# First batch's token products: the part over its first two token tiles and first 256 columns in a job between the two halves

## The chip, the cores and the metric

The kernel runs on one core of a Trainium2 chip. The metric is device time in microseconds (us) of one launch, from first to last instruction with what the launch adds around them. Three runs of the kernel before took 819.28, 820.15 and 820.51 us; the median is 820.15 us.

The engines are called here: PE (TensorE, matrix multiplies and transposes), DVE (VectorE), ACT (ScalarE), POOL (GpSimd) and SP (the queue that issues the transfers). Each takes its own list of instructions in the order in which they are written, and waits for the others through semaphores.

## The reference

Four batches (B = 4) of 576 tokens by 512 channels pass through three layers.

```python
# 1. attention, 8 heads of 64, only scores not below the 32nd largest of a row are kept
scores = q @ k.T / sqrt(64)
kth    = np.partition(scores, -32, axis=-1)[..., -32:-31]
attn   = softmax(where(scores >= kth, scores, -1e9))
x      = (attn @ v), heads joined                       # 576 x 512
# 2. gate: causal convolution over 5 tokens, sigmoid, times x @ w_val, then w_out
x      = (sigmoid(conv(x)) * (x @ w_val)) @ w_out
# 3. phase mixer
theta  = x @ w_theta
zr, zi = x * cos(theta), x * sin(theta)
y      = w_tok_r @ zr + w_tok_i @ zi                    # products over tokens
u      = x + y
out    = u + max(u @ w_ch, 0)
```

The change concerns the line of `y`, for the first batch.

## The kernel before, in words

**Attention.** A head pair has nine tiles of up to 128 query rows (`seq`, line 132). Batch 0 is split (`SPLIT = (0,)`, line 41): its four head pairs are run first for token tiles 0 and 1 (columns 0 to 255, half x = 0), then for tiles 2, 3 and the remaining 64 rows (columns 256 to 575, half x = 1). `COLS` (line 110) holds the two column ranges, `SETS` (line 1053) the token tiles of each half.

The loop at line 1373 takes one tile per step. In a step the functions of `SOON` or `STEP` (lines 58 to 60) are called in a fixed order, and each writes its instructions: `scores_pe` (PE, three steps ahead, into `ps`), `scores_out` (ACT copies `ps` to `s`, line 572), `pick` (DVE, eight largest values of six stretches, lines 594 to 600), `count` (ACT, line 607, which needs the `tops` that `pick` made), `below` (POOL, line 615), `rest` (DVE, line 621), `expo` (ACT, line 202), `mask` (DVE, line 676), `turn` (PE transposes into `pt`) and `turn_out` (ACT copies `pt` to `pT`, line 708). `close` ends a part: sums of the rows, the product of `pT` with v into `px` (line 780), and on DVE `px` times the reciprocal sums `rb` into `xT` (line 798).

**The layers behind.** They are generators in the list `jobs`: `front` (w_val, w_out, theta, and the products z of x with cosine and sine, DVE line 990) and `back` (token products into `py`, line 1134; channel product `ph`; output). `work` runs the first job of the list while `owed` nanoseconds last; a job says what it costs and pauses with `yield paid()`, or stops the step with `yield "sync"` when something isn't there. The budget of a step comes from `target`, which walks a list of `stages` (line 1215), each a cost and a fixed budget (`HIGH` = 6000) or the base of 4150. A job hands instructions for DVE and ACT to `later`; `run_later` writes them into the next step.

**What sets the order.** DVE and ACT have the order in which the program writes (`FIXED`, line 33). PE, POOL and SP are ordered by a scheduler from the priorities of the instructions. Whatever sets it, the order is fixed before the launch, and an engine does not skip an instruction that waits.

**Buffers.** Matrix results of the layers (`px`, `pconv`, `pval`, `pth`, `py`, ...) take turns in four banks (tag `m`), scores in two banks (`s`), transposes in two (`pt`).

**Token products before.** In `back(0)` each of the four channel groups m and each column half h gets one accumulation of nine matrix products, four over token tiles 0 and 1 (z_0) and five over tiles 2, 3 and the rest (z_1). A row group of such products carries f32 operands; the trace shows each as two rows. The token weights w_tok come as 128-row pieces that are converted by ACT, DVE and POOL while attention runs, one piece every two steps; `lacking` counts those not yet there.

Of the kernel before, what the change touches and what calls it, by code (L numbers as in the profile page):

```python
# [11 lines left out]
F32 = mybir.dt.float32  # L12
# [5 lines left out]
ALU = mybir.AluOpType  # L18
# [22 lines left out]
SPLIT = (0,)  # L41
# [49 lines left out]
def mixer(ctx, tc, qT, kT, vt, w_val, conv_t, w_out, w_theta, w_tok, w_ch, out, flag):  # L91
# [269 lines left out]
    def weights():  # L361
        half = DM
        W["raw"] = [ml.tile([P, half, 2], I32, tag=t, name=f"raw_{t}") for t in RAWS]
        W["tmp"] = [ml.tile([P, half], F32, tag=f"lo{x}", name=f"tmp{x}") for x in range(2)]
        pieces = []
        for name, src, factor in (("conv", conv_t, None), ("val", w_val, None), ("out", w_out, None),
                                  ("theta", w_theta, 1.0 / (2.0 * math.pi)), ("tok", w_tok, None), ("ch", w_ch, None)):
            rows, n = src.shape
            W[name] = cp.tile([P, -(-rows // P), n], F32, tag=f"w_{name}", name=f"w_{name}")
            words = src.bitcast(I32).rearrange("r (n t) -> r n t", t=2)  # L370

            chunks = -(-rows // P)
            cuts = [(c, 1, o, o + half) for c in range(chunks) for o in range(0, n - half + 1, half)]
            cuts += [(c, min(8, chunks - c), n // half * half, n) for c in range(0, chunks, 8) if n % half]
            for c, a, o, e in cuts:
                src = words[c * P : (c + a) * P, o:e].rearrange("(a p) n t -> p a n t", a=a)
                lacking[name] = lacking.get(name, 0) + 1
                pieces.append((name, W[name][:, c : c + a, o:e], src, factor, len(pieces)))
        return pieces


# [130 lines left out]
    def after(*keys):  # L512
        while not done.issuperset(keys):
            yield "sync"
# [208 lines left out]
    def close(part):  # L723
# [88 lines left out]
        cw = W["conv"]  # L812
        if hp == NP - 1:
            jobs.append(front(b, (x,) if split else (0, 1)))
            if x:
                jobs.append(back(b))
        yield
# [272 lines left out]
    def fine_tok(w):  # L1090
# [9 lines left out]
        fine["tok", w] = both  # L1100
        halve(*both, W["tok"][:, w, :], ("tok", B - 1, w))

    def back(b):
        x2T = ms.pop(b)

        def y_out(m, h, ps):
            lo, hi = COLS[h]

            def f():
                nc.vector.tensor_tensor(x2T[:, m, lo:hi], ps, x2T[:, m, lo:hi], ALU.add)  # L1110
                if m == NC - 1 and (h or b == B - 1):
                    for k in (h,) if b == B - 1 else range(2):
                        halve_room(b, k, "U", x2T)
                if not h:
                    due.append(m)
                    while due and m % 2 and not lacking["ch"]:
                        want(b, "ch", due.pop(0))
            return f

        due = []  # L1120
        while lacking["tok"]:
            yield "sync"
        if b < B - 1:
            for h, m in [(h, m) for h in range(2) for m in range(NC)]:
                lo, hi = COLS[h]
                yield from after(*[("z", b, i) for i in SETS[0]])
                ps = ps_m.tile([P, hi - lo], F32, tag="m", name=f"py_{b}_{m}_{h}")
                for x in range(2):
                    if x:
                        yield from after(*[("z", b, i) for i in SETS[1]])  # L1130
                    for i in SETS[x]:
                        zs = [(cos_of(b, i), i), (sin_of(b, i), i + NF + 1)] if i < NF else [(sin_of(b, i), NF)]
                        for k, (z, w) in enumerate(zs):
                            nc.tensor.matmul(ps, z[:, m * P : (m + 1) * P], W["tok"][:, w, lo:hi],  # L1134
                                             start=(i + k == 0), stop=(i == NF))
                            owe[0] += (hi - lo) * 1.675
                            if owe[0] >= GRAIN and i < NF:
                                yield paid()
                later.append(y_out(m, h, ps))
                yield paid()  # L1140
        else:
            for h in range(2):
                lo, hi = COLS[h]
                ps = [ps_m.tile([P, hi - lo], F32, tag="m", name=f"py_{b}_{m}_{h}") for m in range(NC)]
                for x, n in ((0, 0), (1, 0), (0, 1), (1, 1)):
                    for m in range(NC):
                        for i in SETS[x]:
                            for k, (_, w) in enumerate(mixed(b, i)):
                                yield from after(("cs"[k], b, i), ("tok", b, w))
                                z = fine_z(i, k)[n][:, m * P : (m + 1) * P]  # L1150
                                for t in fine["tok", w][: 2 - n]:
                                    first = (x, n, i, k) == (0, 0, 0, 0) and t is fine["tok", w][0]
                                    nc.tensor.matmul(ps[m], z, t[:, lo:hi], start=first, stop=n == 1 and i == NF)  # L1153
                                owe[0] += (hi - lo) * 0.425 * (2 - n)
                                if owe[0] >= GRAIN and i < NF:
                                    yield paid()
                        if x and n:
                            later.append(y_out(m, h, ps[m]))
                        yield paid()

        def h_out(m, h, ps):
            lo, hi = COLS[h]

            def f():
                nc.vector.scalar_tensor_tensor(x2T[:, m, lo:hi], ps, 0.0, x2T[:, m, lo:hi], ALU.max, ALU.add)
                n = b + 1
                if h and n in THREE:
                    if m % 2:
                        want(n, "val", m)
                    if (n * NP + m, 0) in there:  # L1170
                        split_x(n, m, 0)
                done.add(("o", b, m, h))
            return f

        def store(i, w, po):
            def f():
                ot = x2T[:w, :, i * P : i * P + P] if w == P else x2T[:w, :, :P]
                nc.scalar.copy(ot, po[:w])
                nc.sync.dma_start(out[b, i * P : i * P + w, :].rearrange("t (c w) -> t c w", c=NC), ot)
            return f  # L1180

        def turned(tiles):
            for i in tiles:
                w = P if i < NF else REM
                po = ps_m.tile([P, NC, P], F32, tag="m", name=f"po_{b}_{i}")
                for c in range(NC):
                    nc.tensor.transpose(po[:w, c, :], x2T[:, c, i * P : i * P + w], ident)
                later.append(store(i, w, po))
                yield 450

        while lacking["ch"]:
            yield "sync"
        while due:
            want(b, "ch", due.pop(0))
        for h, m in [(h, m) for h in range(2) for m in range(NC)]:
            lo, hi = COLS[h]
            yield from after(*halved(b, h, "U"), ("w", b, "ch", m))
            ps = ps_m.tile([P, hi - lo], F32, tag="m", name=f"ph_{b}_{m}_{h}")
            yield from products(ps, [(mat(b, "ch", m, c), chunk(b, h, "U", c)) for c in range(NC)])
            later.append(h_out(m, h, ps))  # L1200
            if (h, m) == (1, NC - 1):
                used(b, "ch")
            yield paid()
            if h and m == 1:
                yield from after(*[("o", b, c, 0) for c in range(NC)])
                yield from turned([0, 1])
        yield from after(*[("o", b, c, 1) for c in range(NC)])
        yield from turned(range(2, NF + 1))
# [7 lines left out]
    for b in range(B):  # L1216
        late = b == B - 1
        f = 1.275 if b in THREE else 1.675
        by = 0 if late else end((b + 1) * NP + 1, 0) + SHIFT[0]
        if b in SPLIT:  # L1220
            for x, (lo, hi) in enumerate(COLS):
                stages.append((2 * NC * (hi - lo) * NC * f + len(SETS[x]) * (NC * DM * f + 500.0), HIGH if x else None, by))
        else:
            stages.append((2 * NC * S * NC * f + 5 * NC * DM * f, HIGH if late else None, by))
        stages.append((NC * S * NC * 1.275 + 36 * S * 1.675 + 5000, HIGH if late else None,
                       0 if late else end((b + 2) * NP - 1, 1) + SHIFT[1]))
    spent_on = [0.0]

# [201 lines left out]
```

## Time and profile before

| | |
|---|---|
| median of three runs | 820.15 us |
| the profiled execution, its own time | 818.77 us |
| its span, first to last instruction | 817.0 us |
| PE busy | 722.8 us (88% of the span) |
| DVE busy | 665.9 us (82%) |
| ACT busy | 633.6 us (78%) |
| POOL busy | 451.4 us (55%) |
| the chain that ended last | PE 43%, DVE 30%, ACT 13%, POOL 6%, DMA 4% |

The busy shares are averages. In the chain that ended last DVE and PE take turns, so a stretch has to be read by itself: which engine has no idle time in it, and for what the others wait. In a row of the timeline the first two numbers are the start and the time that the row covers, `x8` is the number of instructions joined in it, and the bracket says how long the engine was idle before the row and which instruction ended that. Rows of one engine run into each other by some hundredths of a microsecond.

### The profile page before, as it was taken

The numbers are of one execution on the slowest core, as the hardware profiler recorded it, in microseconds if no ns is written. First come the engines' busy times: TensorE is split into PE (matmuls) and PEld (weight loads), VectorE is DVE, ScalarE is ACT, GpSimd is POOL, SyncE is SP. The second block draws the span as 40 slices with busy tenths as digits, with TensorE's granted clock in tenths as the row PEclk, the third lists the DMA queues.
The fourth block names the chain that finished last, engine by engine and source line by source line (L and its number), as shares of the span: only waits on it lengthen the run. The fifth ranks groups of instructions, "written<-read, shape, count | busy, mean of one in ns | idle before, by whom it ended". The sixth has DMA issues, their size and how long they took to land.

```text
span 817.0 us, 15416 instructions
## 1 busy us (share of the span) xinstructions
PE 722.8 (88%) x4478; PEld 580.9 (71%) x4478; DVE 665.9 (82%) x2708; ACT 633.6 (78%) x1517; POOL 451.4 (55%) x557
## 2 busy tenths in 40 slices
PE   5467899958999899996989989999999899999995
PEld 3345577536757676965787767788988677898995
DVE  5999999879977899997999799989988795353522
ACT  6788999889779888998789988889988874346411
POOL 5977676556644454657577445647895251015500
PEclk9998999989999999998889999999999999999998
DMA  5676776545342343276365523325662300070002
GB/s 153 169 181 167 188 185 173 153 112 137 77 129 72 78 145 91 61 221 174 91 182 159 170 75 87 73 73 145 181 185 79 104 16 1 1 244 21 2 1 63
DMA packets 69982, 94.33 MB, mean 115 GB/s; under 512 B 13312, under 2 KB 36736, under 8 KB 69888
## 3 DMA queue, kind: packets, MB, share of 16 engines
q1 hardware_dynamic: 69568, 92.82, 41.7%
q8 instruction: 38, 0.62, 0.3%
q14 instruction: 56, 0.46, 0.2%
q10 hardware_dynamic: 320, 0.43, 0.2%
HBM read 49.96 MB, written 13.11 MB: 77 GB/s over the span
## 4 chain that ended last, share of the span: by engine, by line
PE 43%; DVE 30%; ACT 13%; POOL 6%; DMA 4%; issue 3%; SPq 1%; ACTq 0%; POOLq 0%; DVEq 0%
PE px L780 7%; PE py L1134 7%; DVE cand L594 6%; DVE s L676 5%; DVE thrs L621 4%; PE pval L529 4%; PE px2t L529 4%; PE pth L529 4%; PE ph L529 4%; PE py L1153 3%; PE pt L689 3%; DVE gp L845 2%; DVE cand L600 2%; PE ps L558 2%; DVE tops L598 2%
## 5 line engine op out<-in xcount | busy, mean ns | idle before, releaser
L615 POOL TENSOR_TENSOR y<-s,n 128x576 f32<-128x576 f32 x144 | 188.6, 1309 | 191.9 <-DVE thrs L621 139.4
L594 DVE MAX8 cand<-s 128x8 f32<-128x96 f32 x864 | 210.2, 244 | 6.1 <-ACT s L572 6.1
L676 DVE SCALAR_TENSOR_TENSOR s<-s,thrs,e 128x576 f32<-128x576 f32 x144 | 140.8, 978 | 2.3 <-ACT e L202 2.3
L607 ACT ACTIVATE n<-s,tops 128x576 bf16<-128x576 f32 x144 | 112.0, 778 | 32.0 <-POOL y L615 13.5
L572 ACT ACTIVATE s<-ps 128x256 f32<-128x256 f32 (+1 forms) x288 | 103.4, 405 | 25.3 <-PE ps L693 9.3
L1134 PE MATMUL py<-w_tok,z 128*128 128x256 f32 (+1 forms) x432 | 116.1, 408 | 6.4 <-DVE z L990 6.4
L621 DVE MAX8 thrs<-y 128x8 f32<-128x584 f32 x144 | 109.3, 759 | 5.4 <-POOL y L616 4.8
L202 ACT ACTIVATE e<-s,least 128x576 f32<-128x576 f32 x144 | 110.8, 769 | 1.4 <-POOL gp L837 1.3
L689 PE MATMUL pt<-ident,s 128*128 128x128 f32 x576 | 95.1, 286 | 16.9 <-ACT pT L708 8.0
L689 PEld LDWEIGHTS pt<-ident,s 128*128 128x128 f32 x576 | 69.8, 146 | 43.1 <-ACT pT L708 14.7
L558 PE MATMUL ps<-kh_None,q 128*128 128x256 f32 x240 | 91.9, 390 | 5.5 <-ACT rb L759 2.8
L1134 PEld LDWEIGHTS py<-w_tok,z 128*128 128x128 f32 x432 | 77.4, 190 | 26.4 <-DVE z L990 8.8
L708 ACT COPY pT<-pt 128x512 f32<-128x512 f32 x128 | 73.1, 571 | 23.2 <-PE pt L689 13.5
L780 PE MATMUL px<-pT,v 128*64 128x256 f32 (+1 forms) x512 | 76.6, 435 | 13.4 <-ACT pT L708 13.4
L598 DVE MAX8 tops<-cand 128x8 f32<-128x48 f32 x432 | 82.6, 191 | 0.1
L559 PE MATMUL ps<-kl_None,q 128*128 128x256 f32 x240 | 71.8, 302 | 0.0
L780 PEld LDWEIGHTS px<-pT,v 128*64 128x64 f32 x512 | 34.3, 143 | 44.2 <-ACT pT L708 15.7
L558 PEld LDWEIGHTS ps<-kh_None,q 128*128 128x128 f32 x240 | 46.8, 195 | 20.1 <-ACT s L572 6.5
L558 PE MATMUL ps<-kh,q 128*128 128x256 f32 (+1 forms) x80 | 36.0, 457 | 22.2 <-ACT s L572 9.3
L600 DVE MATCH_REPLACE8 cand<-tops,cand 128x48 f32<-128x48 f32 x288 | 55.0, 191 | 0.0
L559 PEld LDWEIGHTS ps<-kl_None,q 128*128 128x128 f32 x240 | 47.4, 198 | 2.3 <-issue 0.5
L697 ACT COPY pT<-ps 64x128 f32<-64x128 f32 (+1 forms) x160 | 39.1, 245 | 11.9 <-PE ps L693 5.6
(206 smaller groups left out, 1716.3 us busy)
## 6 DMA issues: line engine op xcount, KB each, us to landing
kh_None<-kh_None SPq DMA_DIRECT2D x48, 144.0 KB, 2.7
kl_None<-kl_None SPq DMA_DIRECT2D x48, 144.0 KB, 2.8
v<-in_vt_dram SPq DMA_DIRECT2D x20, 256.0 KB, 3.7
out_dram<-x2T SPq DMA_DIRECT2D x16, 256.0 KB, 2.9
w<-ch SPq DMA_DIRECT2D x16, 256.0 KB, 4.4
w<-theta SPq DMA_DIRECT2D x16, 256.0 KB, 5.4
raw_hi<-in_w_tok_dram SPq DMA_DIRECT2D x7, 512.0 KB, 3.9
kh<-kh SPq DMA_DIRECT2D x24, 144.0 KB, 2.4
```

Source lines behind the costliest of these rows:

```text
L202: ins = nc.scalar.activation(out, src, func, **more).ins
L529: nc.tensor.matmul(ps[o : o + n], x, y, start=(i + k == 0), stop=(i == last and k == len(ways) - 1), skip_group_check=(n < P))
L558: nc.tensor.matmul(bank[:, :w], q2, kh[:, lo:hi], start=(j == js[0]), stop=False)
L559: nc.tensor.matmul(bank[:, :w], q2, kl[:, lo:hi], start=False, stop=(j == js[-1]))
L594: nc.vector.max(d["cand"][:, k, 8 * x : 8 * x + 8], s_tiles[i][:, x * SUB : (x + 1) * SUB])
L607: nc.scalar.activation(n, s_tiles[i], AF.Sign, bias=d["tops"][:, k, KC - 1 : KC], scale=-(1.0 + 2.0 ** -22), accum_out=acc)
L615: nc.gpsimd.tensor_tensor(y[:, :S], s_tiles[i], d.pop(("n", k)), ALU.mult)
L621: nc.vector.max(thrs[:, N - 1 - i : N - 1 - i + NK], d.pop(("y", k)))
L676: nc.vector.scalar_tensor_tensor(p, p, thr(i), e.exp, ALU.is_ge, ALU.mult, accum_out=part["sums"][:, e.slot : e.slot + 1])
L689: nc.tensor.transpose(e.pt[:, c, :], p[:, c * P : (c + 1) * P], ident)
L780: nc.tensor.matmul(px[d, :], of_v, pT[:, k, :], start=(c == 0), stop=(c == NF), skip_group_check=True)
L1134: nc.tensor.matmul(ps, z[:, m * P : (m + 1) * P], W["tok"][:, w, lo:hi], start=(i + k == 0), stop=(i == NF))
```

## The change

- The conversion of w_tok takes the four pieces that belong to token tiles 0 and 1 (chunks 0, 1, 5 and 6) before the others, and counts them as `first`.
- A new job `first_tokens(0)` is put into `jobs` behind `front(0, (0,))`, so ahead of `front(0, (1,))`. For each m it makes the four products of z_0 with the first 256 columns of w_tok into a bank `py_0_m`, and hands DVE an addition of this bank to x2T.
- `back(0)` leaves these four products out of its first column half, and starts that accumulation with z_1. Its own four additions stay, so x2T gets four more additions of 128 x 256 in all.
- `stages` gets an entry of 4 x 4 x 256 x 1.675 = 6861 ns with budget `HIGH` behind the first half, and the entry of `back(0)` is less by the same.

```diff
             cuts += [(c, min(8, chunks - c), n // half * half, n) for c in range(0, chunks, 8) if n % half]
+            if name == "tok":
+                cuts.sort(key=lambda cut: cut[0] % (NF + 1) >= 2 or cut[2] > 0)
             for c, a, o, e in cuts:
...
-                lacking[name] = lacking.get(name, 0) + 1
-                pieces.append((name, W[name][:, c : c + a, o:e], src, factor, len(pieces)))
+                kind = "first" if name == "tok" and o == 0 and c % (NF + 1) < 2 else name
+                lacking[kind] = lacking.get(kind, 0) + 1
+                pieces.append((kind, W[name][:, c : c + a, o:e], src, factor, len(pieces)))
...
             jobs.append(front(b, (x,) if split else (0, 1)))
+            if split and not x:
+                jobs.append(first_tokens(b))
...
+    def first_tokens(b):
+
+        x2T = ms[b]
+        lo, hi = COLS[0]
+
+        def out_of(m, ps):
+            return lambda: nc.vector.tensor_tensor(x2T[:, m, lo:hi], ps, x2T[:, m, lo:hi], ALU.add)
+
+        while lacking["first"]:
+            yield "sync"
+        yield from after(*[("z", b, i) for i in SETS[0]])
+        for m in range(NC):
+            ps = ps_m.tile([P, hi - lo], F32, tag="m", name=f"py0_{b}_{m}")
+            for i in SETS[0]:
+                for k, (z, w) in enumerate(mixed(b, i)):
+                    nc.tensor.matmul(ps, z[:, m * P : (m + 1) * P], W["tok"][:, w, lo:hi], start=(i + k == 0),
+                                     stop=(i + k == 2))
+                    owe[0] += (hi - lo) * 1.675
+            later.append(out_of(m, ps))
+            yield paid()
...
-                for x in range(2):
+                for x in range(b in SPLIT and h == 0, 2):
...
-                                             start=(i + k == 0), stop=(i == NF))
+                                             start=(i + k == (2 if b in SPLIT and h == 0 else 0)),
+                                             stop=(i == NF))
...
+                if not x:
+                    stages.append((NC * 4 * (hi - lo) * 1.675, HIGH, by))
...
+        less = NC * 4 * CUT * 1.675 if b in SPLIT else 0.0
```

Where the job lands on PE, in the second half of batch 0. Before (`px_1` is the product with v of a head pair's second half, `pt` are transposes, the rows of `ps` a tile's scores with the last rows and the sums of an ending part in the same banks):

```order
341 L780 MATMUL px_1_2312<-pT_1_1992,v_last 64x320 x2
342 L689 MATMUL pt_2351<-ident,s_1808 128x128 x4
343 L689 MATMUL pt_2409<-ident,s_1868 128x128 x4
344 L558 MATMUL ps_0_2364<-kh_4_None,q_88 128x256
345 L559 MATMUL ps_0_2364<-kl_4_None,q_88 128x256
346 L693 MATMUL ps_0_2364<-ident,s_1808 64x128
347 L752 MATMUL ps_0_2364<-rT,spread 128x128
348 L558 MATMUL ps_256_2369<-kh_4_None,q_88 128x320
349 L559 MATMUL ps_256_2369<-kl_4_None,q_88 128x320
350 L752 MATMUL ps_256_2369<-rT,spread 128x128
351 L755 MATMUL ps_256_2369<-rT,spread 128x64 x2
352 L689 MATMUL pt_2454<-ident,s_1935 128x128 x4
```

The same place now:

```order
342 L692 MATMUL pt_2351<-ident,s_1808 128x128 x4
343 L1123 MATMUL py_0_0_2364<-w_tok,z_0_2006 128x256 x4
344 L561 MATMUL ps_0_2369<-kh_4_None,q_88 128x256
...
351 L758 MATMUL ps_256_2374<-rT,spread 128x64 x2
352 L1123 MATMUL py_0_1_2380<-w_tok,z_0_2006 128x256 x4
353 L692 MATMUL pt_2419<-ident,s_1868 128x128 x4
354 L1123 MATMUL py_0_2_2432<-w_tok,z_0_2006 128x256 x4
355 L561 MATMUL ps_0_2437<-kh_4_None,q_88 128x256
...
359 L562 MATMUL ps_256_2441<-kl_4_None,q_88 128x320
360 L1123 MATMUL py_0_3_2444<-w_tok,z_0_2006 128x256 x4
361 L692 MATMUL pt_2476<-ident,s_1935 128x128 x4
```

The four groups of products stand among the scores of two tiles, and the second set of transposes (`s_1868`) has moved behind the scores and behind two of the groups.

The additions on DVE, at the same steps (line 679 is the mask, line 624 the last selection of a tile, line 801 `px` times `rb`; between line 624 and line 340 stands the selection of a tile):

```order
592 L679 SCALAR_TENSOR_TENSOR s_1935,sums_1_2203<-s_1935,thrs,e_2346 128x576
593 L1114 TENSOR_TENSOR x2T_1697<-py_0_0_2364,x2T_1697 128x256
594 L1114 TENSOR_TENSOR x2T_1697<-py_0_1_2380,x2T_1697 128x256
595 L624 MAX thrs<-y_2394 128x8
596 L597 MAX cand_2327<-s_2356 128x8
...
607 L340 TENSOR_SCALAR tmp_132<-tmp_132 128x512
608 L679 SCALAR_TENSOR_TENSOR s_1998,sums_1_2203<-s_1998,thrs,e_2414 128x576
609 L341 TENSOR_SCALAR tmp_132<-tmp_132 128x512
610 L801 TENSOR_TENSOR xT_1171<-px_1_2312,rb_1_2216 128x320
611 L1114 TENSOR_TENSOR x2T_1697<-py_0_2_2432,x2T_1697 128x256
612 L1114 TENSOR_TENSOR x2T_1697<-py_0_3_2444,x2T_1697 128x256
613 L624 MAX thrs<-y_2450 128x8
```

Two additions stand ahead of the selection of the tile `s_2356`, two ahead of the next tile's; the rest of DVE's order is as before there.

The start of `back(0)` on PE now; before, four z_0 products of `py_0_0` stood ahead of its z_1 products, and those of `py_1` and `py_2` among them:

```order
523 L562 MATMUL ps_256_3322<-kl_6_None,q_88 128x320
524 L1160 MATMUL py_0_0_3445<-w_tok,z_1_3074 128x256 x4
525 L692 MATMUL pt_3415<-ident,s_2868 128x128 x3
526 L561 MATMUL ps_0_3370<-kh_6_None,q_88 128x256
527 L562 MATMUL ps_0_3370<-kl_6_None,q_88 128x256
```

The first product now reads z_1. From the first product of batch 1 (`pval`) on, PE's order is again the one before, but for a shift by one or two rows.

## Rows read from the trace of the kernel before

**Rows 1.** Busy time by stretch: length, PE, PEld, DVE, ACT, POOL busy, clock, DMA.
```profile
176.80:184.40 7.60, 5.77 (x41) 4.02 (x38) 4.27 (x21) 5.94 (x16) 2.59 (x4) 1.00 0.40 113
184.40:201.00 16.60, 13.64 (x74) 8.95 (x73) 16.60 (x83) 16.19 (x41) 10.78 (x13) 0.90 0.53 141
193.20:258.70 65.50, 63.41 (x345) 42.99 (x345) 56.15 (x253) 53.63 (x130) 36.52 (x49) 0.97 0.38 104
268.60:376.00 107.40, 100.02 (x653) 79.05 (x652) 105.00 (x453) 93.71 (x237) 60.00 (x73) 0.98 0.47 129
```

**Rows 2.** Timeline of POOL and DVE: the fourth token piece, and z_0.
```profile
164.33 1.49 POOL L354 TENSOR_TENSOR w_tok<-raw_hi 128x512 int32<-128x512 int32 x1 [0.79 <-ACT z L969]
...
168.57 2.48 DVE L990 TENSOR_TENSOR z<-px,z 128x512 f32<-128x512 f32 x4
```

**Rows 3.** Timeline of DVE where the additions are put in.
```profile
176.01 0.82 DVE L676 SCALAR_TENSOR_TENSOR s<-s,thrs,e 128x576 f32<-128x576 f32 x1
...
176.76 0.76 DVE L621 MAX8 thrs<-y 128x8 f32<-128x584 f32 x1
179.93 0.26 DVE L594 MAX8 cand<-s 128x8 f32<-128x96 f32 x1 [2.41 <-ACT s L572]
...
184.00 0.49 DVE L798 TENSOR_TENSOR xT<-px,rb 128x320 f32<-128x320 f32 x1 [0.92 <-ACT rb L759]
184.40 0.76 DVE L621 MAX8 thrs<-y 128x8 f32<-128x584 f32 x1
...
186.45 0.20 DVE L598 MAX8 tops<-cand 128x8 f32<-128x48 f32 x1
```

**Rows 4.** Timeline of PE from the place of the new products on.
```profile
178.26 0.66 PE L689 MATMUL pt<-ident,s 128*128 128x128 f32 x4
...
180.27 0.38 PE L558 MATMUL ps<-kh_None,q 128*128 128x256 f32 x1 [0.52 <-ACT s L572]
...
181.46 0.56 PE L755 MATMUL ps<-rT,spread 128*128 128x64 f32 x4
...
183.80 0.38 PE L558 MATMUL ps<-kh_None,q 128*128 128x256 f32 x1 [0.83 <-ACT rb L759]
...
184.56 2.95 PE L827 MATMUL pconv<-xT,diagonals 128*128 128x320 f32 x10
...
193.24 2.27 PE L780 MATMUL px<-pT,v 128*64 128x320 f32 x8 [1.61 <-ACT pT L708]
...
196.90 1.30 PE L780 MATMUL px<-pT,v 128*64 128x320 f32 x8
```

**Rows 5.** Timeline of ACT: the count of three tiles (line 607).
```profile
183.83 0.81 ACT L607 ACTIVATE n<-s,tops 128x576 bf16<-128x576 f32 x1
...
187.36 0.78 ACT L607 ACTIVATE n<-s,tops 128x576 bf16<-128x576 f32 x1
...
190.85 0.78 ACT L607 ACTIVATE n<-s,tops 128x576 bf16<-128x576 f32 x1
```

**Rows 6.** Timeline of PE: the first token products of batch 0.
```profile
255.04 1.89 PE L1134 MATMUL py<-w_tok,z 128*128 128x256 f32 x8
258.74 3.52 PE L1134 MATMUL py<-w_tok,z 128*128 128x256 f32 x14 [1.81 <-DVE z L990]
```

**Rows 7.** Timeline of DVE: its waits from 212 to 300, and an addition.
```profile
214.36 0.49 DVE L874 SCALAR_TENSOR_TENSOR gp<-gp,pval 128x320 f32<-128x320 f32 x1 [1.83 <-PE pval L529]
...
262.46 0.26 DVE L594 MAX8 cand<-s 128x8 f32<-128x96 f32 x1 [1.31 <-ACT s L572]
...
265.79 0.82 DVE L676 SCALAR_TENSOR_TENSOR s<-s,thrs,e 128x576 f32<-128x576 f32 x1 [0.99 <-ACT e L202]
...
268.61 1.67 DVE L845 SCALAR_TENSOR_TENSOR gp<-xT,w_conv,gp 128x576 f32<-128x576 f32 x2 [2.00 <-POOL gp L837]
...
275.31 0.42 DVE L1110 TENSOR_TENSOR x2T<-py,x2T 128x256 f32<-128x256 f32 x1
...
298.08 1.12 DVE L415 TENSOR_TENSOR lo_-1_3823<-w_ch,hi_-1_3822 128x512 fp32r<-128x512 f32 x1 [1.68 <-ACT hi_-1_3822 L411]
```

More of the change, by code (lines that the diff above doesn't have):

```diff
@@ L1120, in back @@
         due = []
-        while lacking["tok"]:
+        while lacking["tok"] or lacking["first"]:
             yield "sync"
@@ L1222, in mixer @@
                 stages.append((2 * NC * (hi - lo) * NC * f + len(SETS[x]) * (NC * DM * f + 500.0), HIGH if x else None, by))
+                if not x:
+                    stages.append((NC * 4 * (hi - lo) * 1.675, HIGH, by))
         else:
             stages.append((2 * NC * S * NC * f + 5 * NC * DM * f, HIGH if late else None, by))
-        stages.append((NC * S * NC * 1.275 + 36 * S * 1.675 + 5000, HIGH if late else None,
+        less = NC * 4 * CUT * 1.675 if b in SPLIT else 0.0
+        stages.append((NC * S * NC * 1.275 + 36 * S * 1.675 + 5000 - less, HIGH if late else None,
                        0 if late else end((b + 2) * NP - 1, 1) + SHIFT[1]))
```

## The prediction

> **What bounds the kernel now.** I read the busy time by stretch first, then the timeline of DVE, PE and ACT at the two places where products leave and arrive, and at each wait what ended it.
>
> Between 184.4 and 201.0 DVE is busy 16.60 of 16.60 us and ACT 16.19, PE only 13.64 [rows 1]: attention's selection on DVE, and ACT beside it, set the pace. Just ahead, 176.8 to 184.4, all three have gaps. From 193.2 to 258.7 PE is busy 63.41 of 65.50, DVE has 9.35 us free, and where DVE waits at 214.36 it waits for a product (`pval`) [rows 1, 7]: there PE is the bound. From 258.7 DVE waits three times, 1.31, 0.99 and 2.00 us, each ended by ACT or POOL and none by PE [rows 7]; from 268.6 to 376.0 it has 2.40 us free in 107.40, of which one wait for ACT's copy of w_ch is 1.68 [rows 1, 7]. So the stretch from which products are taken is bound by DVE and ACT, and the stretch into which they go is tight on DVE and ACT too, with the gaps on PE.
>
> **What moves.** Sixteen products of 128 x 256. Four of them are one row of eight instructions, 1.89 us [rows 6]; all are 4 x 1.89 = 7.56 us of PE. DVE gets four additions; one is 0.42 [rows 7], 0.33 net of the 0.09 by which a DVE row runs into the next (184.00 + 0.49 against 184.40 [rows 3]), so 1.3 us. Operands are no wait: the fourth piece of w_tok is done at 165.8 and z_0 at 171.1 [rows 2], both ahead of 178. The reordered conversion has the same steps and durations, and its transfers change places on SP only behind these four: nothing.
>
> **Where they arrive.** I push the rows of before through the new order, in times of before. PE: the transposes start at 178.26; one group of four lets the next instruction start 0.45 to 0.5 later, so `py_0_0` runs 178.8 to 180.7. The scores behind it could start at 180.27 and now start at 180.7; up to the sums they take 182.02 - 180.27 = 1.75, less a tail of 0.1 under the next [rows 4]. `py_0_1` runs from 182.3 to 184.2.
>
> DVE ends the mask started at 176.01 and now meets two additions. The second needs `py_0_1`, and the selection (line 621 before) is queued behind it: it starts at 184.2 + 0.33 = 184.55 and not at 176.76. Of these 7.8 us DVE idled 2.41 + 0.92 anyway [rows 3]. From 176.76 to line 798 at 184.00 there are 7.24 - 3.33 = 3.9 us of work, so line 798 starts at 188.45, and ends at 188.85.
>
> `py_0_2` runs at about 184.65 to 186.55, behind transposes; scores of 0.76 follow (183.80 to 184.56 [rows 4]), until 187.3. `py_0_3` wants the bank of `px`, which line 798 frees: 188.85 + 1.89 = 190.75. Additions three and four stand behind line 798, the fourth waits for that product, and the next selection starts at 191.1 instead of 184.40: 6.7 us late, 1.3 of it the additions' own time, the rest waiting.
>
> ACT's counts need the selection's `tops`. Before, they are ready at 186.65, 2.25 after the selection's start [rows 3], and the count begins at 187.36, 0.71 later [rows 5]. Now they are ready at 191.1 + 2.25 = 193.35, so the count is 6.0 late, and with DVE full the next at 190.85 is as late. Behind ACT stands `px` on PE, which at 193.24 had waited 1.61 us for ACT's copy pT [rows 4]: no cover is left there, and PE is about 6.1 late where the stretch that it bounds itself begins. DVE's 9.35 us free in that stretch buy nothing, since they are waits for PE.
>
> The bounds: 6.7 (DVE's lag all of it) above. [...] I take 5.7: the same wait of 1.6 us for pT still stands ahead of `px`, and ACT, which is full, would stop a faster PE soon, so about a quarter of the gain. [...]
>
> **Where they leave.** Of 7.56 us, 1.89 filled PE while it waited for z_1: the row at 255.04 ends at 256.9, and 1.81 of waiting is left [rows 6]. Now PE waits from 255.04 to 258.74. So 5.67 us of PE work go from behind 258.74. I cost this at nothing: DVE's waits in the stretch end with ACT and POOL [rows 7], which don't wait for these products, and behind 268.6 DVE is full. What is late next, once the products are gone, is DVE's selection, as before. The wait for w_ch (1.68) stands a step or two earlier in the new order; it could go or double, so between -1.7 and +1.7, and I take 0 since copy and subtraction keep their order. If PE's clock falls in the longer wait, four products at half speed cost another 1.89; 5.67 us less work covers that.
>
> `back(0)` is done about 6861 / 4150 = 1.65 steps earlier, but batch 1's first product keeps its place in PE's order, where it waits for attention of batch 1. Nothing is gained there.
>
> **Sum.** The profiled execution took 818.77 us (span 817.0, and 1.77 around it); with 5.7 it is 824.5. It lies 1.38 under the median of 820.15, to which the prediction is compared: 825.9.
>
> **Rivals.**
> *The products taken out pay as well.* If PE bounded 258.7 to 300, the 5.67 us would come back: 825.9 - 5.7 = 820.2, no change. For it: PE is busy in most of that stretch. Against: the four waits of DVE (5.98 in sum) would have to end on PE, and all end elsewhere [rows 7]. It decides at the additions of `back(0)`: they would have to start by that much earlier.
> *PE sets the end all through, faster.* One mechanism: DVE's and ACT's lag at 191 does not reach PE, because they run ahead enough, and is made up in their 9.35 us free before 258.7. Then only PE's own time counts: 7.56 put in, less the gaps there (1.83 in 176.8 to 184.4, 2.96 in 184.4 to 201.0 [rows 1]) and less the 1.66 of low clock, is 1.1; 5.67 come off later; 4.6 faster, 815.6. It decides at `px` (193.24 before): if ACT's pT is there in time, this case holds. Against it: PE waits 1.61 for just that copy already, and counts start 0.7 behind their selection. [...]
> *Only the additions count.* If the scheduler's place is harmless because `py_0_1` and `py_0_3` are done when DVE gets there, 1.3 us of DVE are left: 821.5. Against it: `py_0_1` stands behind the scores and `py_0_3` behind line 798 in the new order.
>
> **How the numbers follow.** Slower by the stall 0.74, its own range 824.5 (4.4) to 828.8 (6.7 with 1.89 of low clock not covered); the products pay too 0.12; only additions 0.05; PE sets the end 0.09. A measurement of this kernel can tell 0.2%, 1.6 us. The second and third fall within it, so faster 0.09, same 0.17, slower 0.74. The range reaches from 818.6, the lower edge of no change, to 829.0; outside lie the faster case and about 0.05 above.
>
> **What would show it.** Right: on DVE two pairs of additions with idle time before them, ended by PE `py`, together some 7 us at 177 to 191, of which the waits at 179.93 and 184.00 have vanished; the selection that started at 184.40 starts near 191; ACT's counts wait for `tops` there; batch 1's `pval` and everything from 200 on about 6 late. PE waits near 3.7 us for z_1 ahead of the first `py` of `back(0)`, at a start 5 to 6 later than 255, and DVE is as full from 270 to 376 as now. Wrong: the additions start without idle time, or `px` behind 193 without waiting for ACT; or the lag at 255 is there and gone at 300, which is the first rival.

## The result, and the profile after

The kernel now takes 827.09 us (median of 4 runs, 826.81 to 827.34), against 819.72 for the kernel before in the same comparison (4 runs). The ratio is 1.0089, 95% interval 1.0071 to 1.0106: slower by 5.8 to 8.7 us. The forecast was 825.9. The profiled execution took 827.34, with a span of 825.5 against 817.0, so 8.5 us have to be found.

To find them I compare the start of the same instruction in both traces: attention has 144 masks on DVE (line 676 before, 679 now), counted here from 0. The lag is the start now less the start before. It is -0.24 at tile 34, 4.66 at tile 36, 4.14 at tile 64 (320.30 before), 8.50 at tile 84 (408.49 before) and 8.50 at the last. There are two losses: one of 4.1 to 4.7 where the products arrive, and one of 4.4 behind 320; in between 0.5 comes back. (From tile 64 to 84 the lag stands as high as 12.3, because DVE does some of its work earlier now. At tile 84 it has nearly the same behind it in both traces, 1624 instructions before and 1627 now.)

**First loss.** DVE around the job, answering to [rows 3] (the bracket is the idle time before the row, and what ended it):

```profile
175.77 0.82 DVE L679 SCALAR_TENSOR_TENSOR s<-s,thrs,e 128x576 f32<-128x576 f32 x1
...
180.69 0.42 DVE L1114 TENSOR_TENSOR x2T<-py,x2T 128x256 f32<-128x256 f32 x1 [4.09 <-PE py L1123]
183.95 0.42 DVE L1114 TENSOR_TENSOR x2T<-py,x2T 128x256 f32<-128x256 f32 x1 [2.84 <-PE py L1123]
184.29 0.76 DVE L624 MAX8 thrs<-y 128x8 f32<-128x584 f32 x1
...
188.00 0.48 DVE L801 TENSOR_TENSOR xT<-px,rb 128x320 f32<-128x320 f32 x1
188.41 0.75 DVE L1114 TENSOR_TENSOR x2T<-py,x2T 128x256 f32<-128x256 f32 x2
189.07 0.76 DVE L624 MAX8 thrs<-y 128x8 f32<-128x584 f32 x1
```

The first pair of additions waits 4.09 and 2.84 us for its products; the second pair waits for nothing. These 6.93 us stand in place of the 2.41 and 0.92 that DVE waited before; with the 1.3 of the additions' own time that makes 4.9, the step of the lag from -0.24 to 4.66. The selection that stood at 184.40 starts at 189.07.

PE in the same place, answering to [rows 4], the job's four products and the next head pair's `px`:

```profile
178.75 1.89 PE L1123 MATMUL py<-w_tok,z 128*128 128x256 f32 x8
181.97 1.95 PE L1123 MATMUL py<-w_tok,z 128*128 128x256 f32 x8
184.18 1.89 PE L1123 MATMUL py<-w_tok,z 128*128 128x256 f32 x8
186.55 1.89 PE L1123 MATMUL py<-w_tok,z 128*128 128x256 f32 x8
...
197.50 2.40 PE L783 MATMUL px<-pT,v 128*64 128x320 f32 x8 [1.84 <-ACT pT L711]
```

The fourth product starts at 186.55, ahead of line 801 at 188.00. `px` is 4.26 later than at 193.24, and still waits for ACT. ACT's counts, answering to [rows 5], are 2.79, 4.04 and 4.27 late:

```profile
186.62 0.78 ACT L610 ACTIVATE n<-s,tops 128x576 bf16<-128x576 f32 x1 [2.69 <-DVE tops L601]
191.40 0.78 ACT L610 ACTIVATE n<-s,tops 128x576 bf16<-128x576 f32 x1 [1.30 <-DVE tops L601]
195.12 0.78 ACT L610 ACTIVATE n<-s,tops 128x576 bf16<-128x576 f32 x1 [0.25 <-POOL y L619]
```

PE's busy time (the first of the five) and its granted clock (behind the fifth), across the job and in the stretch that answers to [rows 1]:

```profile
176.60:189.10 12.50, 12.50 (x78) 10.49 (x75) 5.58 (x24) 7.95 (x20) 2.60 (x4) 1.00 0.22 69
189.10:205.70 16.60, 13.61 (x78) 8.89 (x76) 16.60 (x83) 14.53 (x37) 10.82 (x13) 0.90 0.63 168
```

**Where products were taken out.** PE before the first `py` of `back(0)`, answering to [rows 6], and DVE's three waits that answer to [rows 7]:

```profile
262.88 3.75 PE L1160 MATMUL py<-w_tok,z 128*128 128x256 f32 x8 [3.62 <-DVE z L995]
```
```profile
266.50 0.26 DVE L597 MAX8 cand<-s 128x8 f32<-128x96 f32 x1 [1.30 <-ACT s L575]
269.83 0.82 DVE L679 SCALAR_TENSOR_TENSOR s<-s,thrs,e 128x576 f32<-128x576 f32 x1 [1.00 <-ACT e L202]
272.67 1.67 DVE L850 SCALAR_TENSOR_TENSOR gp<-xT,w_conv,gp 128x576 f32<-128x576 f32 x2 [2.00 <-POOL gp L842]
```

PE waits 3.62 us, and the eight instructions behind it take 3.75 where they took 1.89, under a granted clock of 0.50 and not 1.00. DVE's waits are what they were (1.31, 0.99, 2.00), and the lag stays at 4.06 to 4.04 across them. Here less work on PE brings nothing, and its slower start costs nothing.

**Second loss.** DVE, ACT and PE at the channel stage of batch 0 now. U is x2T split into a rounded part (four casts on ACT) and a rest (four subtractions on DVE), from which PE makes the channel products `ph`:

```profile
326.53 2.77 DVE L418 TENSOR_TENSOR U<-x2T,U 128x512 fp32r<-128x512 f32 x4 [1.28 <-ACT U L414]
...
336.45 0.42 DVE L1192 SCALAR_TENSOR_TENSOR x2T<-ph,x2T 128x256 f32<-128x256 f32 x1 [0.74 <-PE ph L532]
338.53 0.42 DVE L1192 SCALAR_TENSOR_TENSOR x2T<-ph,x2T 128x256 f32<-128x256 f32 x1 [1.65 <-PE ph L532]
...
343.36 0.42 DVE L1192 SCALAR_TENSOR_TENSOR x2T<-ph,x2T 128x256 f32<-128x256 f32 x1 [1.03 <-PE ph L532]
```
```profile
325.23 0.76 ACT L202 ACTIVATE e<-s,least 128x576 f32<-128x576 f32 x1
325.89 2.37 ACT L414 CAST U<-x2T 128x512 fp32r<-128x512 f32 x4
328.17 0.57 ACT L711 COPY pT<-pt 128x512 f32<-128x512 f32 x1
```
```profile
328.80 1.30 PE L783 MATMUL px<-pT,v 128*64 128x320 f32 x8 [3.27 <-ACT pT L711]
331.58 2.29 PE L783 MATMUL px<-pT,v 128*64 128x320 f32 x8
```

Four waits on DVE, 4.70 us together, of which the kernel before has none. The same rows of the kernel before:

```profile
327.85 2.76 DVE L415 TENSOR_TENSOR U<-x2T,U 128x512 fp32r<-128x512 f32 x4
...
338.28 0.74 DVE L1165 SCALAR_TENSOR_TENSOR x2T<-ph,x2T 128x256 f32<-128x256 f32 x2
...
341.99 0.74 DVE L1165 SCALAR_TENSOR_TENSOR x2T<-ph,x2T 128x256 f32<-128x256 f32 x2
```
```profile
324.72 2.37 PE L780 MATMUL px<-pT,v 128*64 128x320 f32 x16
```

Before, DVE subtracts at 327.85, behind the mask of tile 66, and no bracket stands at U or `ph`. The 16 products `px` of that head pair's second half end at 327.09, as ACT's casts begin (327.02). Now U stands behind the mask of tile 64: two tiles earlier, because `back(0)` has less to do. There ACT's casts stand ahead of the copy pT, and PE waits 3.27 us for that copy. Less the lag of 4.14, `px` starts at 324.66, as before; but scores that ran ahead of it (`ps`, at 323.64 to 324.72 before) now stand behind its first half, and its second half starts at 327.44, when before all of it was done. `ph` comes later by that, while DVE's additions behind `ph` are two tiles earlier.

DVE's busy time by stretch shows it too. The row of the kernel before, then one of now across the second loss:

```profile
321.00:338.00 17.00, 16.39 (x121) 13.71 (x119) 17.00 (x73) 16.96 (x46) 8.71 (x11) 1.00 0.28 74
```
```profile
325.00:346.00 21.00, 17.73 (x127) 14.76 (x126) 16.30 (x73) 16.32 (x41) 6.96 (x9) 0.92 0.21 55
```

Third and fourth of the five busy times are DVE and ACT: DVE was busy 17.00 of 17.00, and is now busy 16.30 of 21.00. The clock granted to PE is 0.92 there, not 1.00.

### The profile page after: what moved, and what is told of

Same layout as the page of the kernel before. It is cut to its first block, busy times and chain, and to the rows that moved or that the text cites. A ratio compares the mean times of both kernels' runs of the same rounds, so it can differ in the third digit from the quotient of the medians.

```text
span 825.5 us, 15416 instructions
## 1 busy us (share of the span) xinstructions
PE 725.5 (88%) x4478; PEld 583.0 (71%) x4478; DVE 669.5 (81%) x2712; ACT 634.8 (77%) x1517; POOL 452.4 (55%) x557
## 4 chain that ended last, share of the span: by engine, by line
PE 46%; DVE 29%; ACT 12%; POOL 5%; issue 3%; DMA 2%; SPq 1%; ACTq 0%; POOLq 0%; DVEq 0%
PE py L1160 7%; PE px L783 7%; DVE cand L597 6%; DVE s L679 5%; PE pth L532 5%; PE px2t L532 4%; DVE thrs L624 4%; PE ph L532 4%; PE pval L532 4%; PE pt L692 3%; PE py L1180 3%; PE ps L561 2%; DVE gp L850 2%; DVE cand L603 2%; DVE tops L601 2%
## 5 line engine op out<-in xcount | busy, mean ns | idle before, releaser
L1160 PE MATMUL py<-w_tok,z 128*128 128x320 f32 (+1 forms) x400 | 110.1, 416 | 8.6 <-DVE z L995 8.6
L1160 PEld LDWEIGHTS py<-w_tok,z 128*128 128x128 f32 x400 | 73.1, 194 | 27.9 <-DVE z L995 6.9
```

## The experiments

Each starts from the changed kernel. Ratios are to the kernel before on the same chip. Its median was 818.47 us beside job_only, back_only, charge_kept and adds_step_later, 817.94 beside casts_behind_turn, and 818.96 beside the other four. The times expected count from the 819.72 and 827.09 of the result, so what compares is the time over the kernel before. The lags of the profiled executions, in us:

```
kernel               tile 34   38     64     84    last   ratio [95%]
the change            -0.24   4.66   4.14   8.50   8.50   1.0089 [1.0071, 1.0106]
job_only              -0.67   4.54   4.09   3.98   4.52   1.0055 [1.0041, 1.0069]
back_only             -0.38   0.49  -0.02   4.78   4.75   1.0062 [1.0048, 1.0076]
charge_kept           -0.56   4.61   4.13   4.08   3.44   1.0050 [1.0037, 1.0064]
adds_step_later       -0.33   1.62   1.05   1.10   0.56   1.0013 [1.0004, 1.0022]
u_step_later          -0.38   5.63   5.13   5.96   6.12   1.0072 [1.0058, 1.0086]
u_two_later            0.77   5.65   5.09   4.79   4.80   1.0067 [1.0045, 1.0089]
channel_step_later    -0.61   4.24   5.32   7.12   8.43   1.0099 [1.0084, 1.0115]
adds_and_u_later      -0.11   1.23   1.15   0.28  -0.32   1.0013 [1.0003, 1.0024]
casts_behind_turn     -0.51   4.50   4.04   4.33   6.54   1.0084 [1.0064, 1.0104]
```

**job_only**: the job and its additions, while `back(0)` still makes all its products (z_0 is counted twice).

```diff
-                for x in range(b in SPLIT and h == 0, 2):
+                for x in range(2):
...
-        less = NC * 4 * CUT * 1.675 if b in SPLIT else 0.0
+        less = 0.0
```

> One part of the change alone: the new job with its sixteen products and four additions stays, and back(0) keeps all its products and its pace, so the z_0 part is counted twice. Theory of two losses (the trace after shows the masks 4.1 us late at the first token products of back(0) and another 4.4 us late by 400): this kernel loses only the first, about +4.3 over before, 824.0 (823 to 825). Rival of one loss (what is lost later follows from the shift made at the job): the whole +7.4, 827. By the prediction's own sum (+5.7 at the job, nothing later): 825.4.

823.32 us. The first loss alone, 4.09 at tile 64; no second one (3.98 at tile 84).

**back_only**: the products are left out of `back(0)` and made nowhere.

```diff
-            if split and not x:
-                jobs.append(first_tokens(b))
...
-                if not x:
-                    stages.append((NC * 4 * (hi - lo) * 1.675, HIGH, by))
```

> The other part alone: no new job, its stage left out; back(0) leaves the four products of z_0 out of its first column half (they are made nowhere: sixteen products less work) and is done earlier, as in the change. Theory of two losses: although it does 7.56 us less on PE it is slower than before, since the split of U and the channel product fall on other steps, where DVE waits for ACT's copies and for ph: +4.2, 823.9 (822.5 to 825). Rival of one loss: nothing late without the job, so not slower: 819.7 or up to 1.5 less.

823.68 us: slower than before with 16 products less. The lag is -0.02 at tile 64 and 4.78 at tile 84, with the waits of the changed kernel almost to the hundredth. DVE, then PE, of this kernel:

```profile
322.37 2.77 DVE L418 TENSOR_TENSOR U<-x2T,U 128x512 fp32r<-128x512 f32 x4 [1.28 <-ACT U L414]
332.28 0.42 DVE L1190 SCALAR_TENSOR_TENSOR x2T<-ph,x2T 128x256 f32<-128x256 f32 x1 [0.72 <-PE ph L532]
334.35 0.42 DVE L1190 SCALAR_TENSOR_TENSOR x2T<-ph,x2T 128x256 f32<-128x256 f32 x1 [1.65 <-PE ph L532]
...
339.19 0.42 DVE L1190 SCALAR_TENSOR_TENSOR x2T<-ph,x2T 128x256 f32<-128x256 f32 x1 [1.03 <-PE ph L532]
```
```profile
324.65 2.40 PE L783 MATMUL px<-pT,v 128*64 128x320 f32 x8 [3.27 <-ACT pT L711]
```

So the second loss does not need the first. The lag of -0.02 at tile 64, behind the stretch from which the products are gone, also shows that they pay nothing there.

**charge_kept**: the change, but `back(0)` goes on charging its budget for the four products, and so keeps its pace over the steps.

```diff
+                if b in SPLIT and h == 0:
+                    for _ in range(4):
+                        owe[0] += (hi - lo) * 1.675
+                        if owe[0] >= GRAIN:
+                            yield paid()
...
-        less = NC * 4 * CUT * 1.675 if b in SPLIT else 0.0
+        less = 0.0
```

> The change, but back(0) still charges the four products that it no longer makes (and its stage entry is not reduced), so that everything behind is written into the same steps as before; DVE's order is that of before plus the four additions. Theory of two losses: the second goes, +4.2 stays: 823.9 (822.5 to 824.8). Rival of one loss: as the change, 827. If the products taken out paid at all, up to 5.67 less: 818.5 to 820.

822.61 us. With the pace kept, the second loss is gone (4.13, then 4.08), though PE does the same work as in the change: it is the place in the order that costs, not the products.

**adds_step_later**: charge_kept, with the job's four additions written one step later.

```diff
-            later.append(out_of(m, ps))
+            later.append(lambda f=out_of(m, ps): later.append(f))
```

> As charge_kept, and each of the four additions is written one step later than in the change; PE's order is the same through all sixteen products. Theory (the first loss is DVE held in its order by additions that come before their products are done): the wait goes, the additions' own 1.3 us and some tenths on ACT are left: 821.0 (820.3 to 822.0). Rival (the loss is PE's 7.56 us put between scores and transposes, whoever waits for it): as charge_kept, 823.9, at best 1 us less.

819.44 us, 1.0 over the kernel before. DVE of this kernel:

```profile
184.29 0.49 DVE L801 TENSOR_TENSOR xT<-px,rb 128x320 f32<-128x320 f32 x1 [0.91 <-ACT rb L762]
184.70 0.75 DVE L1114 TENSOR_TENSOR x2T<-py,x2T 128x256 f32<-128x256 f32 x2
...
189.11 0.72 DVE L1114 TENSOR_TENSOR x2T<-py,x2T 128x256 f32<-128x256 f32 x2
```

No addition waits. What is left at tile 64 is 1.05, so of the 4.13 of charge_kept 3.1 were waiting in order, and about 1.1 the additions themselves.

**u_step_later** and **u_two_later**: the change, with the splitting of U written one or two steps later.

```diff
-                    for k in (h,) if b == B - 1 else range(2):
-                        halve_room(b, k, "U", x2T)
+                    def halves():
+                        for k in (h,) if b == B - 1 else range(2):
+                            halve_room(b, k, "U", x2T)
+                    if b in SPLIT:
+                        later.append(lambda: later.append(halves))
+                    else:
+                        halves()
```

(This is two steps; one step has `later.append(halves)`.)

> The change, with the splitting of U of batch 0 (four casts on ACT, four subtractions on DVE) written one step later; all products and additions are kept. In the changed kernel the casts (2.37 us) stand on ACT just ahead of the copy pT for which PE's px waits 3.27 us, the U subtraction waits 1.28, and the additions behind ph wait 0.74, 1.65 and 1.03. Theory A (the second loss is made by where U's casts land on ACT): one step later px has its pT, these waits go, the lag of the masks stays near 4.1 from 270 to the end, and the time is 827.1 - 4.4 = 822.7. Rival B (the additions behind ph come too soon behind their products, wherever U lands): only the 1.28 goes, 825.8. Rival C (DVE pays the second loss in any order because the work is only moved): 827.

> The change, with the splitting of U of batch 0 written two steps later, which is the tile of attention at which it stood in the kernel before; the rest is kept. Theory A (place of U's casts on ACT): 822.7, with no wait for U or ph and a lag of 4.1 from the first loss alone. Rival B (the additions behind ph come too soon): 825.8. Rival C: 827. If one step later and two steps later differ by over 1 us, the step itself decides and not the delay.

825.02 and 823.78 us. The lag at tile 64 is 5.1 in both, one more than in the change, and U, which comes later, has no part in that. In u_two_later the one is there ahead of the job (0.77 at tile 34); from there to tile 64 it loses 4.3, as the change does. In u_step_later `px` ahead of the job took 3.47 and not 2.43, and the first addition waits 5.23 and not 4.09:

```profile
175.22 3.47 PE L783 MATMUL px<-pT,v 128*64 128x320 f32 x12
```

From tile 64 to the last mask the first loses 0.99 and the second nothing (-0.29), against 4.36 in the change. In both, PE waits 0.98 for pT and not 3.27 (the row is u_two_later's), and `ph` is not waited for; one step later a wait of 1.13 for U remains, two steps later none.

```profile
327.50 1.30 PE L783 MATMUL px<-pT,v 128*64 128x320 f32 x8 [0.98 <-ACT pT L711]
```

Theory A holds by where the lag stands, and rival B falls. The times show less: they are 6.1 and 4.8 over the kernel before, where 3.0 was expected, and the intervals of both ratios overlap that of the change.

**channel_step_later**: U stays where the change puts it; the additions behind `ph` come one step later.

```diff
-            later.append(h_out(m, h, ps))
+            later.append((lambda f=h_out(m, h, ps): later.append(f)) if b in SPLIT else h_out(m, h, ps))
```

> The change, with the additions behind the channel products ph of batch 0 written one step later; U stays where the change puts it. Theory A says that U's casts start the second loss and that the in-order additions behind ph pass most of it on: the three waits for ph (3.42 us) go, the wait for U (1.28) stays, lag at the end near 5.4, time 823.7 to 824. Rival C (PE is late anyway, so DVE waits next for ACT's or PE's copies of scores): 826.5 to 827.

827.22 us: no gain in time, as rival C had it. The three waits for `ph` are gone, PE's wait for pT is the same 3.27, and DVE now waits in other places:

```profile
327.74 2.77 DVE L418 TENSOR_TENSOR U<-x2T,U 128x512 fp32r<-128x512 f32 x4 [1.29 <-ACT U L414]
...
339.88 0.78 DVE L1192 SCALAR_TENSOR_TENSOR x2T<-ph,x2T 128x256 f32<-128x256 f32 x2
343.98 0.49 DVE L801 TENSOR_TENSOR xT<-px,rb 128x320 f32<-128x320 f32 x1 [0.28 <-ACT rb L762]
...
349.59 0.49 DVE L1192 SCALAR_TENSOR_TENSOR x2T<-ph,x2T 128x320 f32<-128x320 f32 x1 [0.38 <-PE ph L532]
```

In this execution the lag grows by 3.1 from tile 64 to the last mask, and not by 4.4, but it stood 1.2 higher at tile 64 already. So, unlike at the job, the additions are mainly where PE's lateness shows, and my theory that most of the loss is passed on by them is wrong; whether they pass on a part stays open.

**casts_behind_turn**: the change, with pT ahead of U's casts on ACT in that one step.

```diff
+    behind = []
...
-        mid.append(higher)
+        (behind if key[:2] == ("U", 0) else mid).append(higher)
...
+    def run_behind():
+        now, behind[:] = list(behind), []
+        run(now)
...
-        "turn_out": lambda i: inside(i - LAG - TO - 1, turn_out),
+        "turn_out": lambda i: (inside(i - LAG - TO - 1, turn_out), run_behind()),
```

> The change, with one thing altered at its second loss: in the step where ACT makes U's casts for batch 0, the copy pT stands ahead of the four casts instead of behind them (0.57 us against 2.37); nothing else is moved. U's step, the subtraction on DVE and the additions behind ph keep their places. Theory A (the casts ahead of pT hold PE's px, and PE comes late to ph): PE's wait for pT of 3.27 falls by 2.37 to 0.9, px runs 1.30 and not 2.40, DVE's wait for U grows from 1.28 to about 1.8, the waits for ph shrink; second loss near 2.5 instead of 4.4, time 825. Rival D (DVE's wait for U at its own place is what counts, and PE's wait only accompanies it): the wait for U grows by 0.5 and all else stays, 827.5.

825.12 us. PE, then DVE, of this kernel:

```profile
326.41 2.37 PE L784 MATMUL px<-pT,v 128*64 128x320 f32 x16 [0.97 <-ACT pT L712]
```
```profile
326.91 2.76 DVE L419 TENSOR_TENSOR U<-x2T,U 128x512 fp32r<-128x512 f32 x4 [1.76 <-ACT U L415]
```

PE's wait is 0.97, the 16 products `px` take 2.37 as before, and no addition waits for `ph`, though DVE's wait for U grew from 1.28 to 1.76. The lag is 8.0 at tile 72 (12.2 in the change), and back at 4.33 at tile 84, so across the stretch 0.3 is lost, not 4.4: rival D falls. But it grows again to 6.54, in steps between tiles 87 and 124. One of them, 1.1 at tile 96, the change has too: DVE waits there for ACT's `gp`, 1.47 here, 1.46 in the change and 0.41 before. The cause of the others I did not find. The ratio can't be told from that of the change. The time is 7.2 over the kernel before on that chip, where 5.3 was expected; that it meets the 825 of theory A is luck, since the loss at its place is 0.3 and not 2.5. What is shown is the mechanism at its place, and not a remedy.

**adds_and_u_later**: the additions one step later and U two steps later, both as above.

> The change with both remedies: the job's four additions one step later and U's splitting two steps later. If the two losses are separate and the removed products pay nothing: 827.1 - 3.2 - 4.4 = 819.5, about 1 over before, the additions' own time. If the 5.67 us taken from PE pay once nothing spoils them: 818 or less. If one remedy makes the other useless: 822 to 824.

820.25 us (818.36 to 822.40), ratio 1.0013, the same as in adds_step_later, where the second loss was taken away by keeping the pace. Both losses are gone. The profiled execution, the fastest of 11, ends 0.32 ahead of before: behind tile 64 it gained 1.47. Over all runs this is no gain: it is slower than before by 0.2 to 2.0 us, and no version here beats the kernel before.

## Why the prediction was right in sign, and where its steps were off

- **The stall where the products arrive: right in mechanism, too large.** Additions that wait in order for PE, the selection behind them, ACT's counts behind the selection, `px` behind ACT's pT: each link is in the trace, and adds_step_later takes 3.1 of 4.1 us away by taking the waits away. The first pair came as computed (second addition at 184.2 computed, 183.95 measured), and the idle time of some 7 us as well, 6.93, though all of it at the first pair. The step that failed is "`py_0_3` wants the bank of `px`, which line 798 frees: 188.85". It started at 186.55, ahead of line 801. Which bank it had no row shows; that of `py_0_0` was free from 181.1. The second pair therefore waited for nothing, and the selection is 4.7 late instead of 6.7, the counts 4.0 and 4.3 instead of 6.0, `px` 4.3 instead of 6.1.
- **A quarter of the clock's loss won back: no.** That the steps' 6.1 became 5.7, and that the range begins at 4.4, was my estimate, and no run shows the term behind both: 1.66 us that PE's clock could give back, worked out as 16.60 x 0.10 from the 0.90 of [rows 1] (the rival at 815.6 takes it off too). What the run showed in its place: PE was granted 1.00 while it ran the job (176.6 to 189.1), and then 0.90 again from 189.1 to 205.7, the average of [rows 1]; `px` took 2.40 there, under 0.50. A busier stretch ahead saved nothing, and the first loss is near 4.4 because the stall is smaller.
- **PE's own bound behind 193.** "DVE's 9.35 us free buy nothing": right. The lag is 4.66 at tile 38 and 4.14 at tile 64.
- **The removal at 258.7: right there.** PE's wait of 3.62 (3.7 computed), slower products behind it (1.86 more; 1.89 computed) and DVE's unchanged waits all came, and the lag did not move.
- **The wait for w_ch at nothing, within 1.7.** It went from 1.68 to 0.95, 0.73 less; the lag does not show it as a gain (4.04 at tile 52, 4.14 at tile 64).
- **"`back(0)` is done about 6861 / 4150 = 1.65 steps earlier [...] Nothing is gained there": this step failed.** I asked only what could be gained, and looked at batch 1's first product. What `back(0)` hands to the other engines moved as well: U's four casts on ACT and subtractions on DVE came two tiles earlier, into the step where a head pair ends. The casts (2.37) stand ahead of pT there; PE waits 3.27 for it, with scores behind it in its queue, runs half of `px` in 2.29 us and not 1.30, comes late to `ph`, and DVE waits for U and `ph`. It cost 4.4 us. charge_kept, u_two_later and casts_behind_turn each take it away at its place by a different edit; back_only makes it without the job. How much of the 4.4 comes from the slower `px` (2.29 for 1.30) and how much from the order, no run separates.
- The forecast of 5.7 was thus a first loss of 4.1 sized 1.6 too large, and a second of 4.4 sized at nothing. The two errors partly cancel, and 2.8 are left between the profiled executions. The median came only 1.2 above 825.9, because the medians lie 7.4 apart, where the two profiled executions lie 8.6 apart, and the kernel before came out at 819.72, not 820.15. That the sum is so near is to this extent luck.
- **Rivals.** "The products taken out pay too" is refuted by back_only, with its lag of -0.02 at tile 64. "PE sets the end all through" falls at `px`, which waited 1.84 for pT. "Only the additions count" (821.5) describes adds_step_later: with no wait, 1.1 us are left.

## What to carry to other kernels

A job that is made shorter arrives earlier at everything that it issues behind it, on every engine: list those instructions, look at what stands behind them in each queue at the new place, and price a shift that is not asked for. A consumer that is written into an in-order queue one step after its producer is late by whatever the producer lacks: here DVE's additions waited 4.09 and 2.84 us, and one step more took away 3.1 of 4.1 us. Where work is taken from an engine that others wait for only now and then, check at those waits first, since its busy share (88% here) tells nothing of them.

## What the runs showed of the hardware

After a wait of 3.62 us PE ran eight products of 128 x 256 in 3.75 us instead of 1.89, under a granted clock of 0.50 and not 1.00. After the wait of 3.27 us for pT, one half of `px` took longer than the other, and which one differed: 1.30 and then 2.29 in the change, under 1.00 and 0.55, and 2.40 and then 1.30 in back_only. After waits of 0.97 and 0.98 us (casts_behind_turn, and the three kernels in which U comes later) the 16 products took 2.37 together, as in the kernel before, or 1.30 for each half.
